# Batch 1's first DFT stage inside batch 0's pairs, V spread by matmuls, four filter parts

## The chip, the cores and the metric

The kernel runs on one core of one Trainium2 chip. The metric is the device time of one execution in microseconds (us), here the median of several runs. The profile is of one further execution.

## The reference

The input x has 8 batches of 3136 positions by 256 channels. Two blocks follow each other:

```python
X = np.fft.rfft(x, axis=1)
Y = X * (filt_r + 1j * filt_i)[None]          # 1569 frequencies x 256 channels
y = np.fft.irfft(Y, n=3136, axis=1)           # a global filter over the positions

h = y.transpose(0, 2, 1) @ U @ V              # U 3136x32, V 32x3136
u = y + h.transpose(0, 2, 1)
out = u + np.maximum(u @ w_ch1, 0) @ w_ch2    # 256 -> 1024 -> 256
```

Inputs and output are float32; the kernel computes in float16 with float32 accumulation.

## The kernel before

The 3136 positions are split as 64 q by 49 r, and the DFT is done in stages by matmuls. The first stage ("f1") is a DFT over q: matmuls of chunks of x (`xt`) with the constant `w64`. The second is a DFT over r, with twiddles, for 32 frequency groups s; it uses the table `t2` (98 rows, 128 columns for each s) and gives `px`. A pair m handles s = 2m and 2m + 1, so there are 16 pairs. VectorE (DVE) multiplies `px` by the filter tile `ft` (line 408 or lines 419 and 421, `uv`). The inverse of the second stage uses the table `g12` (`pi`); the inverse of the first one uses `s2` within `u_part`. `ft` holds the real filter rows in its first half and the imaginary rows in its second; partitions 64 to 127 get a copy of partitions 0 to 63 (`swap_filters`, line 188) and a negated copy (line 189).

Batch 0 is done at the start, on its own. `first_f1` makes the transposed first stage, `first_a` transposes it back for each pair, and `first_mid` runs the 16 pairs: the product on DVE, `back` (line 313, eight matmuls) for the pair before, `forward` two pairs ahead, `first_a` three pairs ahead. ScalarE (ACT) copies the results of `back` (line 316, `et`) and of `first_a` (line 296, `a`) out of PSUM. After the pairs comes a stage of 13 steps, called the e2 stage here: four transposes on TensorE (line 346), then a copy to `e2`, by ACT and DVE in turn (lines 350 and 352). Into each of these 13 steps one unit of batch 1's f1 is put (`next(fill)`): a matmul (line 366) and a copy by ACT or DVE (lines 372 and 370) to `asb`; after the last unit of a chunk SyncE (SP) stores the chunk in DRAM (`c1`, line 376). Two matmul steps, `h1_unit(0)` (line 467) and `make_u(0)` (lines 490 and 495), lead to the main loop.

The main loop goes over groups of four r, seven groups in an odd batch and six in an even one. Each group has eight matmul pairs `mm1` (line 527) with a ReLU (lines 532 and 534), the eight-step `mm2` of the group before (lines 549 and 553), its copy to `och` (line 558) and two stores to `out` (line 565). `make_u` of the next group stands in the middle. The other batches' DFT work is spread over this loop by slots, eight in a group of four: `put(slot, gen)` fixes which unit runs where. Batch 1's pairs start at slot 9, with `load_a(1, 0)`, the load of the stored first stage, at slot 3.

The order on every engine is the program's order (`manual_schedule`), and the DMA queues of SP and GpSimd (POOL) issue in that order too. POOL issues the loads that convert to float16: x of batch 0 (eight loads), all parts of the filters (`load_filters`, lines 162 to 179), U, x of batch 1, V, `w1`, `w2`, `s2`, x of batch 2. SP issues the tables (`load_tables`, line 157), all of them before the pairs. V is loaded four times, to partitions 0, 32, 64 and 96, in two halves, and POOL copies it to `vrs` in the order that `u_part` needs (`prep_v`, line 228).

Of the kernel before, what the change touches and what calls it, by code (L numbers as in the profile page):

```python
# [16 lines left out]
DM = 256  # L17
# [8 lines left out]
def _consts():  # L26
    n, half = SEQ, SEQ // 2
    r = np.arange(NR)
    q = np.arange(NQ)


    w = np.zeros((NQ, NS, 2))
    for s in range(NS):
        w[:, s, 0] = np.cos(2 * np.pi * s * q / NQ)
        w[:, s, 1] = -np.sin(2 * np.pi * s * q / NQ)
    w[:, 0, 1] = (-1.0) ** q
    w = w.reshape(NQ, 64)
    w64 = np.zeros((128, 128))
    w64[:64, :64] = w
    w64[64:, 64:] = w  # L40
    s2 = np.zeros((128, 128))
    s2[:64, :64] = w.T / ESC
    s2[64:, 64:] = w.T / ESC


    t2 = np.zeros((NS, 98, 128))
    g = np.zeros((NS, 128, 98))
    for s in range(NS):
        for j in range(49):
            if j < 25:  # L50
                f = s + 64 * j
                e, sg = np.exp(-2j * np.pi * f * r / n), 1.0
            elif s:
                f = 64 * (j - 24) - s
                e, sg = np.exp(-2j * np.pi * (n - f) * r / n), -1.0
            else:
                f = 32 + 64 * (j - 25)
                e, sg = np.exp(-2j * np.pi * f * r / n), 1.0
            ei = np.conj(e)
            if s:  # L60
                t2[s, :49, j], t2[s, 49:, j] = e.real, -e.imag
                t2[s, :49, 64 + j], t2[s, 49:, 64 + j] = sg * e.imag, sg * e.real
                g[s, j] = np.concatenate([ei.real, ei.imag]) * 2
                g[s, 64 + j] = np.concatenate([-ei.imag, ei.real]) * 2 * sg
            else:
                o = 0 if j < 25 else 49
                t2[s, o:o + 49, j] = e.real
                t2[s, o:o + 49, 64 + j] = e.imag
                g[s, j, o:o + 49] = ei.real * (2 if f else 1)
                g[s, 64 + j, o:o + 49] = -ei.imag * 2  # L70

    t2[0, :, 64] = 0
    t2[0, 49:, 64] = (-1.0) ** r
    g[0, 64] = 0
    g[0, 64, 49:] = (-1.0) ** r
    g *= ESC / n
    gs = np.concatenate([g[:, 64:], g[:, :64]], 1)
    f16 = np.float16
    return (w64.astype(f16), s2.astype(f16), np.eye(128).astype(f16),
            np.ascontiguousarray(t2.transpose(1, 0, 2).reshape(98, NS * 128)).astype(f16),  # L80
            np.ascontiguousarray(np.stack([g, gs], 1).transpose(2, 0, 1, 3)
                                 .reshape(128, NS * 2 * 98)).astype(f16))
# [3 lines left out]
def kernel(  # L86
# [10 lines left out]
):  # L97
    nc = tc.nc
    nb = x.shape[0]
    w64_np, s2_np, idn_np, t2_np, g_np = _consts()  # L100
    w64_d = nc.inline_tensor(w64_np, name="w64d")
    s2_d = nc.inline_tensor(s2_np, name="s2d")
    idn_d = nc.inline_tensor(idn_np, name="idnd")
    t2_d = nc.inline_tensor(t2_np, name="t2d")
    g_d = nc.inline_tensor(g_np, name="gd")
    RD = NR * DM
# [38 lines left out]
    g12 = cst.tile([128, NS * 2 * 98], F16)  # L145
    ft = cst.tile([128, 2 * NS * DM], F16)
    nyq = cst.tile([65, DM], F16)
    PARTS = ((0, 4), (4, 8), (8, 16), (16, 24), (24, 32))
    for a, b in PARTS:
        for c in (0, NS * DM):  # L150
            nc.vector.memset(ft[32:64, c + a * DM:c + b * DM], 0.0)
# [28 lines left out]
                nyq[64:65, :],  # L180
                bass.AP(tensor=filt_r.tensor, offset=(SEQ // 2) * DM, ap=[[DM, 1], [1, DM]]))

    def swap_filters(a, b):

        fb = NS * DM
        if a == 0:
            nc.vector.memset(ft[0:1, fb:fb + DM], 0.0)
        nc.vector.tensor_copy(ft[64:128, a * DM:b * DM], ft[0:64, a * DM:b * DM])
        nc.vector.tensor_scalar_mul(ft[64:128, fb + a * DM:fb + b * DM],
                                    ft[0:64, fb + a * DM:fb + b * DM], -1.0)  # L190
        if a == 0:
            nc.vector.tensor_copy(ft[64:65, 0:DM], nyq[64:65, :])

    for a, b in PARTS:
        load_filters(a, b)
    uq = sb.tile([64, NR * RANK], F16, tag="esb", bufs=2, name="uq")
    nc.gpsimd.dma_start(uq, moe_U.rearrange("(q r) p -> q (r p)", q=NQ))
    for c in range(len(CH)):
        load_x(1, c)
    vqs = []  # L200
    for k in range(2):
        v = sb.tile([128, SEQ // 2], F16, tag="och", bufs=2, name="vq")
        vqs.append(v.rearrange("p (q r) -> p r q", r=NR))
        for j in range(4):
            nc.gpsimd.dma_start(v[32 * j:32 * j + 32, :], moe_V[:, k * (SEQ // 2):(k + 1) * (SEQ // 2)])
    w1 = cst.tile([128, 2 * 1024], F16)
    nc.gpsimd.dma_start(w1, moe_w_ch1.rearrange("(h dd) c -> dd h c", h=2))
    w2 = cst.tile([128, 8 * DM], F16)
    nc.gpsimd.dma_start(w2, moe_w_ch2.rearrange("(t cc) e -> cc t e", t=8))
    s2 = cst.tile([128, 128], F16)  # L210
    nc.gpsimd.dma_start(s2, s2_d.ap())
    VR = ((0, 8), (8, NH))
    vrs = [cst.tile([128, (b - a) * 128], F16, name=f"vr{a}") for a, b in VR]

    def v_at(r):
        k = r >= VR[1][0]
        return vrs[k], (r - VR[k][0]) * 128
    usb = cst.tile([128, NH * RANK], F16)
    nc.vector.memset(usb[64:128, (NH - 1) * RANK:NH * RANK], 0.0)

    def prep_v(part):

        a, b = VR[part]
        dst = vrs[part].rearrange("p (r h q) -> p h r q", h=2, q=NQ)
        for h in range(2):
            w = min(b, NH - h) - a
            for k, v in enumerate(vqs):
                nc.gpsimd.tensor_copy(dst[:, h, 0:w, k * 32:k * 32 + 32],
                                      v[:, h * NH + a:h * NH + a + w, :])

    def new_e2(b):
        e2 = sb.tile([128, NH * DM], F16, tag="e2", bufs=2, name="e2")
# [22 lines left out]
    def first_f1():  # L255
        ne = 0
        xs = [st[0]["x"][c] for c in range(len(CH))]
        for r0 in range(0, NH - 1, 4):
            if r0 == 8:
                load_tables(*PARTS[0])  # L260
            for dh in range(2):
                pa = bank("m", "pa")
                for rr in range(4):
                    c = next(k for k in range(len(CH)) if r0 + rr < c0[k + 1])
                    o = (r0 + rr - c0[c]) * DM + dh * 128
                    nc.tensor.matmul(pa[:, rr * 128:(rr + 1) * 128], xs[c][:, o:o + 128], w64[:, :],
                                     start=True, stop=True, skip_group_check=True)
                for h in range(2):
                    dst = atv[:, dh, :, h * NH + r0:h * NH + r0 + 4]
                    src = pa.rearrange("p (r h k) -> p h k r", h=2, k=64)[:, h]  # L270
                    if ne % 2:
                        nc.vector.tensor_copy(dst, src)
                    else:
                        nc.scalar.copy(dst, src)
                    ne += 1
# [23 lines left out]
    def first_mid(fill):  # L299
# [23 lines left out]

        pxs = [ahead(0), ahead(1)]
        for m in range(NS // 2):
            for part in PARTS[1:]:
                if 2 * m == part[0]:
                    swap_filters(*part)
            uv = both_products(m, pxs.pop(0))
            if pend is not None:  # L330
                back(*pend)
# [2 lines left out]
                pxs.append(ahead(m + 2))  # L334
            if m + 3 < NS // 2:
                first_a(m + 3)
        back(*pend)
        e2 = new_e2(0)
        for n0 in range(0, NH, 2):
# [12 lines left out]
                nc.vector.tensor_copy(dst, pt[0:k, 0:w * DM])  # L352
            if n0 == 6:
                prep_u()
            next(fill)

    def f1_units(b, both):
        ne = 0
        for c in range(len(CH)):
            xt = st[b]["x"].pop(c)  # L360
            asb = sb.tile([128, 7 * DM], F16, tag="asb", bufs=4, name="asb")
            for n0 in range(0, CH[c], 2):
                w = min(2, CH[c] - n0) * DM
                k = 64 if c0[c] + n0 == NH - 1 else 128
                pf = bank("fx"[ne % 2] if b == 1 else "m", "pf")
                nc.tensor.matmul(pf[0:k, 0:w], w64[0:k, 0:k], xt[0:k, n0 * DM:n0 * DM + w],  # L366
                                 start=True, stop=True)
                dst = asb[0:k, n0 * DM:n0 * DM + w]
                if both and ne % 2:
                    nc.vector.tensor_copy(dst, pf[0:k, 0:w])  # L370
                else:
                    nc.scalar.copy(dst, pf[0:k, 0:w])  # L372
# [112 lines left out]
    def u_part(b, r0, nr, half, pm, o, dh):  # L485

        e2, h1 = st[b]["e2"], st[b]["h1"]
        k = 64 if half else 128
        v, a = v_at(r0)
        nc.tensor.matmul(pm[:, o:o + nr * k], h1[:, dh * 128:(dh + 1) * 128],  # L490
                         v[:, a:a + nr * k], start=True, stop=False,
                         skip_group_check=True)
        for rr in range(nr):
            a = (r0 + rr) * DM + dh * 128
# [41 lines left out]
    def mm2(gx, rr):  # L536
# [22 lines left out]
        if rr == nr - 1:  # L559
            for h in range(2):  # L560
                if nr == 1:
                    dst = rows(out, b - 1 + h, r0 * DM, DM)
                else:
                    dst = rows(out, b, (h * NH + r0) * DM, nr * DM)
                (nc.gpsimd if b < nb - 1 else nc.sync).dma_start(dst, och[64 * h:64 * h + 64, 0:nr * DM])  # L565

    sched = {}

# [10 lines left out]
    SB = 48  # L579

    first_f1()
    for part in PARTS[1:]:
        load_tables(*part)
    swap_filters(*PARTS[0])
    for m in range(3):
        first_a(m)
    for part in range(2):
        prep_v(part)
        for c in range(2):
            load_x(2, 2 * part + c)  # L590
    fill = f1_units(1, True)
    first_mid(fill)
    next(h1_unit(0))
    make_u(0)
# [11 lines left out]
    for b in range(1, nb):  # L606
# [4 lines left out]
        if b > 1:  # L611
            fill = f1_units(b, b == 2)
            for k in range(NF):
                put(1.2 * k if b == 2 else steps[NP * (b - 1)] - 49 + 3 * k, fill)
            for c in range(len(CH)):
                if b > 2:
                    put(steps[NP * (b - 1)] - 68 + 10 * c, one(load_x, b, c))

    slot = 0
    for gx in range(len(groups) + 1):  # L620
# [47 lines left out]
```

## Time and profile before

| | us |
|---|---|
| median of 3 runs (565.89 to 567.01) | 566.82 |
| the profiled execution | 567.93 |
| its span, first to last instruction | 566.2 |

| engine | busy us | share of the span |
|---|---|---|
| PE (matmul) | 527.5 | 93% |
| DVE | 371.4 | 66% |
| ACT | 360.1 | 64% |
| POOL | 248.7 | 44% |

The page's row of PE in 40 slices begins with 3656889 and is 9 from there to the slice before the last; a slice is 14.2 us. The granted TensorE clock is 6 tenths in the third slice and 8 in the fourth of the digits that are not 9 (9968999...), so the low digits stand near 28 to 57 us. The DMA engines are 80% busy or more through the first 70 us. A busy share counts the time in which an instruction is under way; matmuls overlap, so a busy PE is not a PE at its peak. In the views, "idle before" is the time for which the engine had nothing to do before the instruction, and behind the arrow stands what ended it.

### The profile page before, as it was taken

To read this page: it belongs to the slowest core of one execution; us is meant where nothing else is said; L and a number is where in the kernel's file an instruction comes from. 1 tells how busy PE (TensorE), PEld (TensorE's weight loads), DVE (VectorE), ACT (ScalarE), POOL (GpSimd) and SP (SyncE) were. 2 spreads that over 40 slices of the span, in tenths; PEclk is the share of its full clock that TensorE was granted. 3 is DMA by queue.
4 is the path that set the end of the run, shared out by engine and by line. 5 is a ranking of instruction groups with operands and counts; after the bars stand their busy time and mean duration, and the time that the engine had idled before them with its cause. 6 is when DMAs were issued, how large, how long until landed. Compare 5 with 4: busy or idle time off the path is not lost.

```text
span 566.2 us, 11536 instructions
## 1 busy us (share of the span) xinstructions
PE 527.5 (93%) x4403; PEld 377.0 (67%) x4403; DVE 371.4 (66%) x552; ACT 360.1 (64%) x723; POOL 248.7 (44%) x354
## 2 busy tenths in 40 slices
PE   3656889999999999999999999999999999999996
PEld 3444457767767766767677666767677767766665
DVE  7677556676787667776786567776787578424342
ACT  4546756676767686677767586677766576654441
POOL 6557422154564645554555445454444344210000
PEclk9968999999999999999999999999999999999999
DMA  8999977896797767787887667787766534541223
GB/s 151 194 152 177 246 172 155 197 239 151 167 205 168 174 174 168 183 207 173 177 216 169 138 171 181 170 206 174 170 168 135 145 100 106 133 92 50 75 75 83
DMA packets 68822, 90.41 MB, mean 160 GB/s; under 512 B 6902, under 2 KB 53978, under 8 KB 67872
## 3 DMA queue, kind: packets, MB, share of 16 engines
q0 software_dynamic: 18960, 48.60, 39.8%
q1 hardware_dynamic: 49808, 41.08, 30.3%
q8 instruction: 34, 0.56, 0.4%
q14 instruction: 20, 0.16, 0.1%
HBM read 57.99 MB, written 48.17 MB: 188 GB/s over the span
## 4 chain that ended last, share of the span: by engine, by line
PE 80%; DMA 8%; DVE 5%; ACT 2%; issue 2%; POOL 2%; SPq 0%; ACTq 0%; DVEq 0%; POOLq 0%
PE po L549 30%; PE phh L527 27%; PE pi L436 4%; PE px L400 4%; PE po L553 4%; PE pu L490 4%; PE pu L495 3%; PE pf L366 3%; DMA xt<-in_x_dram 3%; DMA ft<-in_filt_i_dram 2%; DVE uv L421 1%; DVE uv L408 1%; PE ph L467 1%; DMA e<-c 1%; ACT h L534 1%
## 5 line engine op out<-in xcount | busy, mean ns | idle before, releaser
L534 ACT ACTIVATE h<-phh 128x512 f16<-128x512 f32 (+1 forms) x350 | 186.5, 575 | 109.7 <-PE phh L527 109.6
L549 PE MATMUL po<-w,h 128*128 128x256 f16 x1568 | 203.2, 273 | 0.0
L527 PE MATMUL phh<-ut,w 128*128 128x512 f16 x768 | 197.5, 379 | 0.5 <-ACT ut L520 0.2
L424 POOL TENSOR_TENSOR y<-uv 128x512 f16<-128x512 f16 x96 | 110.5, 1151 | 149.4 <-DVE uv L421 79.2
L549 PEld LDWEIGHTS <-h 128*128 128x128 f16 x1568 | 150.0, 98 | 35.8
L421 DVE TENSOR_TENSOR uv<-px,ft 64x512 f16<-64x512 f32 x192 | 132.1, 688 | 2.6
L558 DVE COPY och<-po 128x512 f32<-128x512 f32 x96 | 66.4, 692 | 80.8 <-PE po L553 79.1
L527 PEld LDWEIGHTS <-w 128*128 128x128 f16 x832 | 74.9, 98 | 52.7 <-issue 3.0
L419 DVE TENSOR_TENSOR uv<-px,ft 128x512 f16<-128x512 f32 x96 | 66.0, 688 | 55.3 <-PE px L400 48.3
L440 ACT CAST esb<-pi 98x512 f16<-98x512 f32 x112 | 65.8, 588 | 40.3 <-PE pi L436 32.5
L565 POOL DMA_DIRECT2D out_dram<-och x84 | 45.8, 547 | 67.9 <-DVE och L558 65.2
L400 PE MATMUL px<-a,t 98*128 98x256 f16 x256 | 50.4, 280 | 6.7 <-DMA a<-c 2.4
L372 ACT CAST asb<-pf 128x512 f16<-128x512 f32 (+1 forms) x79 | 44.9, 569 | 15.9 <-PE pf L366 15.5
L520 ACT CAST ut<-pu 128x512 f16<-128x512 f32 x96 | 51.8, 598 | 2.3 <-PE pu L495 2.0
L553 PE MATMUL po<-idn,ut 128*128 128x128 f16 x384 | 52.8, 219 | 0.0
L532 DVE TENSOR_SCALAR h<-phh 128x512 f16<-128x512 f32 (+1 forms) x66 | 42.9, 649 | 14.1 <-PE phh L527 13.7
L408 DVE TENSOR_TENSOR uv<-px,ft 128x1024 f16<-128x1024 f32 x32 | 38.1, 1220 | 10.6 <-PE px L400 10.2
L495 PEld LDWEIGHTS <-e 128*128 128x128 f16 (+1 forms) x400 | 30.9, 97 | 17.7 <-issue 2.4
L490 PE MATMUL pu<-vr,h 128*128 128x512 f16 (+1 forms) x112 | 39.6, 354 | 1.3 <-ACT h L471 0.5
L553 PEld LDWEIGHTS <-ut 128*128 128x128 f16 x384 | 37.6, 98 | 4.3
L495 PE MATMUL pu<-s,e 128*128 128x128 f16 (+1 forms) x400 | 40.3, 218 | 0.0
L400 PEld LDWEIGHTS <-t 98*128 98x128 f16 x256 | 22.7, 100 | 25.0 <-issue 8.8
(69 smaller groups left out, 371.5 us busy)
## 6 DMA issues: line engine op xcount, KB each, us to landing
out_dram<-och POOLq DMA_DIRECT2D x84, 256.0 KB, 4.5
a<-c SPq DMA_DIRECT2D x28, 392.0 KB
c<-esb SPq DMA_DIRECT2D x28, 392.0 KB
xt<-in_x_dram POOLq DMA_DIRECT2D x56, 192.0 KB, 6.3
c<-asb POOLq DMA_DIRECT2D x42, 192.0 KB, 3.2
e<-c SPq DMA_DIRECT2D x28, 200.0 KB
e<-c SPq DMA_DIRECT2D x28, 192.0 KB
out_dram<-och SPq DMA_DIRECT2D x12, 256.0 KB
```

The source lines that it names most:

```text
L400: nc.tensor.matmul(px[:, sl * DM:(sl + 1) * DM], t2[:, s * 128:(s + 1) * 128], a2[:, (2 * ml + sl) * DM:(2 * ml + sl + 1) * DM], start=Tru ...
L419: nc.vector.tensor_mul(uv[:, 0:512], px[:, :], ft[:, a:a + 512])
L421: nc.vector.tensor_mul(uv[p:p + 64, 512:1024], px[q:q + 64, :], ft[q:q + 64, b:b + 512])
L424: nc.gpsimd.tensor_add(y, uv[:, 0:512], uv[:, 512:1024])
L440: nc.scalar.copy(esb[:, ml * 512:(ml + 1) * 512], pi[0:98, :])
L490: nc.tensor.matmul(pm[:, o:o + nr * k], h1[:, dh * 128:(dh + 1) * 128], v[:, a:a + nr * k], start=True, stop=False, skip_group_check=True)
L495: nc.tensor.matmul(pm[:, o + rr * k:o + (rr + 1) * k], e2[0:k, a:a + 128], s2[0:k, 0:k], start=False, stop=(rr == nr - 1), skip_group_chec ...
L527: nc.tensor.matmul(pm[:, 0:w], w1[:, dh * 1024 + t * 128:dh * 1024 + (t + 1) * 128], ut[:, dh * w:(dh + 1) * w], start=(dh == 0), stop=(dh ...
L534: nc.scalar.activation(h[:, 0:w], pm[:, 0:w], RELU)
L549: nc.tensor.matmul(po[:, o:o + DM], hs[gx, t][:, rr * 128:(rr + 1) * 128], w2[:, t * DM:(t + 1) * DM], start=(t == 0), stop=False, skip_gr ...
L553: nc.tensor.matmul(po[:, o + dh * 128:o + (dh + 1) * 128], ut[:, dh * w + rr * 128:dh * w + (rr + 1) * 128], idn[:, :], start=False, stop= ...
L558: nc.vector.tensor_copy(och[:, a:(rr + 1) * DM], po[:, 0:(rr + 1) * DM - a])
```

## The change

Four things are changed.

1. The filters come in four parts (0 to 4, 4 to 12, 12 to 20, 20 to 32) instead of five. Batch 1's first two x chunks are loaded ahead of the last part. The tables are no longer all issued before the pairs: part 1 is, part 2 after pair 0's product and part 3 after pair 4's. The real half's copy to partitions 64 to 127 of parts 1 and 2 moves from DVE to ACT, one pair ahead of its use.
2. Of batch 1's 13 f1 units ten go between batch 0's pairs 6 to 15, with ACT doing their copies, and three stay in the e2 stage. They take PSUM banks of the tag "o" instead of "f" and "x".
3. V is loaded once, in two halves of 32 partitions. Seven units (`v_units`) spread it to 128 partitions by matmuls with a selection matrix `sel` (32 by 128) that reads V with a step of 49 elements; ACT copies the result to `vr`. One unit stands in the e2 stage, six in the slots 1, 3, ..., 11 of the main loop. Batch 2's f1 units go from slots 0 to 14 to slots 4 to 17. POOL's copies (`prep_v`) are gone, and batch 2's x loads follow `s2` directly.
4. The second store of the very last group is issued by ACT instead of SP. The buffers of `asb` are three instead of four.

```diff
-    PARTS = ((0, 4), (4, 8), (8, 16), (16, 24), (24, 32))
+    PARTS = ((0, 4), (4, 12), (12, 20), (20, 32))
...
-    def swap_filters(a, b):
+    def swap_real(a, b, on):
+        (nc.scalar.copy if on else nc.vector.tensor_copy)(ft[64:128, a * DM:b * DM],
+                                                          ft[0:64, a * DM:b * DM])
+
+    def swap_imag(a, b):
         fb = NS * DM
         if a == 0:
             nc.vector.memset(ft[0:1, fb:fb + DM], 0.0)
-        nc.vector.tensor_copy(ft[64:128, a * DM:b * DM], ft[0:64, a * DM:b * DM])
         nc.vector.tensor_scalar_mul(ft[64:128, fb + a * DM:fb + b * DM],
                                     ft[0:64, fb + a * DM:fb + b * DM], -1.0)
...
-    for a, b in PARTS:
+    for a, b in PARTS[:3]:
         load_filters(a, b)
+    for c in range(2):
+        load_x(1, c)
+    load_filters(*PARTS[3])
+    for c in range(2, len(CH)):
+        load_x(1, c)
     uq = sb.tile([64, NR * RANK], F16, tag="esb", bufs=2, name="uq")
     nc.gpsimd.dma_start(uq, moe_U.rearrange("(q r) p -> q (r p)", q=NQ))
-    for c in range(len(CH)):
-        load_x(1, c)
     vqs = []
     for k in range(2):
-        v = sb.tile([128, SEQ // 2], F16, tag="och", bufs=2, name="vq")
-        vqs.append(v.rearrange("p (q r) -> p r q", r=NR))
-        for j in range(4):
-            nc.gpsimd.dma_start(v[32 * j:32 * j + 32, :], moe_V[:, k * (SEQ // 2):(k + 1) * (SEQ // 2)])
+        v = sb.tile([32, SEQ // 2], F16, tag="xt", bufs=8, name="vq")
+        vqs.append(v)
+        nc.gpsimd.dma_start(v, moe_V[:, k * (SEQ // 2):(k + 1) * (SEQ // 2)])
...
-    def prep_v(part):
...
+    def v_units():
+        for r0 in range(0, NH, 4):
+            n, nh = (4, 2) if r0 < NH - 1 else (1, 1)
+            pv = bank("m", "pv")
+            for k, v in enumerate(vqs):
+                nc.tensor.matmul(
+                    pv[:, 0:n * nh * 64].rearrange("p (r h q) -> p r h q", h=nh, q=64)
+                    [:, :, :, 32 * k:32 * k + 32],
+                    sel[:, :],
+                    bass.AP(tensor=v.tensor, offset=v.offset + r0,
+                            ap=[v.ap[0], [1, n], [NH, nh], [NR, 32]]),
+                    start=True, stop=True, skip_group_check=True)
+            nc.scalar.copy(vr[:, r0 * 128:r0 * 128 + n * nh * 64], pv[:, 0:n * nh * 64])
+            yield
...
         for m in range(NS // 2):
-            for part in PARTS[1:]:
-                if 2 * m == part[0]:
-                    swap_filters(*part)
+            for k, part in enumerate(PARTS):
+                if k and 2 * m == part[0]:
+                    if k == 3:
+                        swap_real(*part, False)
+                    swap_imag(*part)
             uv = both_products(m, pxs.pop(0))
...
             if m + 3 < NS // 2:
                 first_a(m + 3)
+            for k, part in enumerate(PARTS):
+                if k in (1, 2) and 2 * m + 2 == part[0]:
+                    swap_real(*part, True)
+                if k > 1 and 2 * m + 12 == part[0]:
+                    load_tables(*part)
+            if m >= 6:
+                next(fill)
...
-            next(fill)
+            if n0 in (10, 14, 18):
+                next(fill)
+            if n0 == 22:
+                next(vgen)
...
-            asb = sb.tile([128, 7 * DM], F16, tag="asb", bufs=4, name="asb")
+            asb = sb.tile([128, 7 * DM], F16, tag="asb", bufs=3, name="asb")
...
-                pf = bank("fx"[ne % 2] if b == 1 else "m", "pf")
+                pf = bank("o" if b == 1 else "m", "pf")
...
-                if both and ne % 2:
+                if both and ne % 2 and (b > 1 or ne >= 10):
...
-                (nc.gpsimd if b < nb - 1 else nc.sync).dma_start(dst, och[64 * h:64 * h + 64, 0:nr * DM])
+                eng = nc.gpsimd if b < nb - 1 else nc.scalar if gx + 1 == len(groups) and h else nc.sync
+                eng.dma_start(dst, och[64 * h:64 * h + 64, 0:nr * DM])
...
     first_f1()
-    for part in PARTS[1:]:
-        load_tables(*part)
-    swap_filters(*PARTS[0])
+    load_tables(*PARTS[1])
+    swap_real(*PARTS[0], False)
+    swap_imag(*PARTS[0])
+    nc.vector.tensor_copy(ft[64:65, 0:DM], nyq[64:65, :])
     for m in range(3):
         first_a(m)
-    for part in range(2):
-        prep_v(part)
-        for c in range(2):
-            load_x(2, 2 * part + c)
+    for c in range(len(CH)):
+        load_x(2, c)
     fill = f1_units(1, True)
+    vgen = v_units()
     first_mid(fill)
...
-                put(1.2 * k if b == 2 else steps[NP * (b - 1)] - 49 + 3 * k, fill)
+                put(4 + 1.1 * k if b == 2 else steps[NP * (b - 1)] - 49 + 3 * k, fill)
...
+    for k in range((NH - 1) // 4):
+        put(1 + 2 * k, vgen)
```

## The prediction

> **What bounds the kernel now.** I read the page first: PE is 93% busy over the span. The windows view then says where the other 7% is. This is PE, PEld, DVE, ACT and POOL busy in us, then the granted clock, the DMA share and GB/s:
>
> ```profile
> 25.70:29.10 3.40, 0.00 (x0) 0.00 (x0) 0.69 (x1) 0.54 (x1) 1.18 (x2) 1.00 1.02 183
> 29.10:32.50 3.40, 0.00 (x0) 0.00 (x0) 0.59 (x1) 0.00 (x0) 0.02 (x1) 0.50 1.01 145
> 32.50:35.90 3.40, 1.92 (x20) 1.85 (x21) 3.30 (x4) 0.74 (x3) 3.40 (x7) 0.50 0.82 125
> ...
> 39.40:42.80 3.40, 2.66 (x40) 2.29 (x38) 3.40 (x4) 2.86 (x9) 1.63 (x4) 1.00 1.09 210
> ...
> 63.67:71.50 7.83, 7.57 (x38) 3.35 (x38) 2.72 (x4) 7.18 (x15) 1.35 (x3) 1.00 0.93 226
> 71.50:75.00 3.50, 1.81 (x15) 1.32 (x14) 0.89 (x2) 0.82 (x2) 0.80 (x2) 1.00 1.07 236
> ```
>
> From 80 us on, PE hardly pauses. The time is lost before that: no compute engine does more than two copies from 25.7 to 31.9 while the DMA engines are full. The timeline names the waits (start, duration, operation, idle before it and what ended that):
>
> ```profile
> 31.91 0.69 DVE L189 TENSOR_SCALAR ft<-ft 64x2048 f16<-64x2048 f16 x1 [4.12 <-DMA ft<-in_filt_i_dram]
> ...
> 33.98 0.84 PE L313 MATMUL pi<-g,uv 128*128 128x98 f16 x8 [8.37 <-DVE uv L408]
> ...
> 41.02 2.35 DVE L408 TENSOR_TENSOR uv<-px,ft 128x1024 f16<-128x1024 f32 x2
> ...
> 50.24 0.55 ACT L316 CAST et<-pi 128x200 f16<-128x200 f32 x2 [0.80 <-PE pi L313]
> ...
> 60.99 0.92 PE L467 MATMUL ph<-e,usb 128*32 128x256 f16 x25 [0.45 <-ACT asb L372]
> ...
> 63.67 1.30 PE L527 MATMUL phh<-ut,w 128*128 128x512 f16 x4 [0.23 <-ACT ut L520]
> ...
> 74.38 0.38 PE L400 MATMUL px<-a,t 98*128 98x256 f16 x2 [1.69 <-DMA a<-c]
> ```
>
> So the opening is a chain: filter rows land; sixteen pairs of `first_mid`, paced by DVE (41.02 is the eleventh, pair 10); the e2 stage (50.8 to 60.99); h1 and `make_u`; main loop from 63.67. The chain view gives the wait, and the DMA view of 17.5 to 27.5 the reason (packets, MB, share of the engines):
>
> ```profile
> 18.01 13.88 DMA ft<-in_filt_i_dram
> ```
>
> ```profile
> q1 hardware_dynamic: 830, 1.77, 71.0%
> q0 software_dynamic: 840, 0.49, 36.2%
> ```
>
> Filters (q0) and tables (q1) pass packet for packet, but the tables take 1.77 MB and the filters 0.49. In the DMA view of 30 to 32.5, the tables done, q0 moves 0.33 MB in 2.5 us. The filters' last issue, at 32.48, lands 4.3 us later, at 36.75.
>
> **Part by part.** The base is the profiled execution: 567.93 us, span 566.2; the median of the timed runs is 566.82, 1.1 lower. 0.2%, about what a measurement tells from no change, is 1.1 us.
>
> *1. Filters and tables by parts.* By their shapes all tables are 2.41 MB and all filters 1.57. Today pair 4 waits until 32 for filters that pass beside 2.1 MB of tables. Afterwards parts 1 and 2 (frequencies 4 to 20) pass beside 1.2 MB. Part 1, which landed at 21.5, is 0.2 MB wider: 1.5 us more at the filters' pace alone (0.13 MB/us), 4.1 at the pace beside tables (0.049); I take 23.7, and four products with their swap end near 29. Part 2: 0.79 MB of filters at 0.13 and 1.2 of tables at 0.23 (2.27 MB moved in those 10 us) are 11.3 us from 15.5, landing near 28; ACT's copy of 1.84 puts pair 6 near 31.3, and pair 9 ends near 36. Part 3 (20 to 32) decides: before it on POOL's queue now stand four x loads of batch 1 (0.197 MB each at the 208 GB/s of 40 to 45 us: 0.95 us, 3.8 together), and on SP's queue the first c1 chunk (0.39 MB at the 338 GB/s of 62 to 64.5: 1.2). Bytes of filters and tables are the same. Some DMA slack goes (share 0.84 from 30 to 35: 0.8 us). Landing: 36.75 + 3.8 + 1.2 - 0.8 = about 41.0; I take 40.5, since the c1 chunk need not be wholly ahead. Bounds: 37 (loads overlap freely) and 46.8 (rival B). The swap of 12 rows on DVE is 1.5 x 0.69 = 1.0, so pair 10 starts at 41.5: 0.5 later than now.
>
> *2. Pairs 10 to 15.* Now 41.02 to 50.80, with a pair of swaps (1.4) between. After: six products at 1.155 start to start are 6.9, to 48.4, without swaps. ACT may be later: from the first back copy at 43.2 it has six pair copies at 0.55, two `a` copies and five f1 copies at 0.48 (7.18 us for 15 copies in the window from 63.67): 6.7, to 49.9. So -0.9. The f1 matmuls (0.22 each) ride on PE, whose share per pair is under DVE's at full clock.
>
> *3. The f1 units leave the e2 stage.* Now 10.15 us from 50.84 to 60.99, alternating e2 and asb copies. After: ACT has six e2 copies, 0.88 of usb, two f1 (0.48 and 0.37) and one vr, 5.1; DVE 4.8; with the first transposes' 0.65 and joints, 6.9. That is -3.3. Steps 1 to 3 move the loop's start to 59.5: -4.2, bounds -7 and +2.1 (rivals A and B), almost 1 us per us of part 3's landing. Next late after that landing: ACT.
>
> *Clock.* PE would idle from about 37 to 42.7. In the trace an idle from 25.7 to 34 left the clock at 0.50 until 39.4, and pairs then ran at 1.69 us start to start (35.36 to 37.05). With f1 (0.43 at that clock) PE has about 9 us from 42.7 for what follows pair 10; if the clock recovers 5.4 us after PE's restart, as there, the pairs end 0.6 to 1.3 later. The e2 stage's 8 us of matmuls at half clock (4 at full) would make it up to 1.1 longer. Of these 2.4 I count 0.4, inside the 6.9. "TensorE: Matmul & The Clock Gate", Part 1, says that one idle window of about 3.4 us halves the clock; the row fits, and by it the whole 2.4 would fall due, the sum being 2.0 worse.
>
> *4. The forward's wait.* The last c1 chunk leaves after n0 = 18, near 56.5, instead of after the stage; with up to the 7 us that it took now (62.06 to 68.9) and 5.4 for the `a` load, px has its operand by 69, and slot 9 comes near 69.5. -1.7 (0 if the x2 loads, now issued earlier, crowd it out); half of the 0.67 that px waits for DVE at 78.79: -0.3.
>
> *5. V.* Eight loads become two, and POOL's eight copies (7.9 us) go: nothing waited for them, so 0. Added: seven selection units, one in the e2 stage (in 3), six in slots 1 to 11. The first group's window shows ACT as its limit: 7.18 of 7.83, against 5.8 of matmul pace (16 x 0.216, 0.86 for `make_u`, 7 x 0.22). There ACT gets four vr copies and two f1 copies fewer: 2 x 0.48 = +1.0. Three f1 units shift into the PE-bound groups, 0.66, with two v units, 0.3. Together +2.0. No row has a moving operand that steps 98 bytes. Nearest is the contiguous one, 0.109 per 256 columns (eight in 0.87), which I take; farthest is POOL's copy of the same V at the same step, 746 ns per 256 elements (against 576 for its contiguous add, 1151 per 512). At that pace four units in the first group bring PE there from 5.2 (three f1 fewer) to 11.2, 3.0 over ACT's 8.2, and the later units cost 1.6 more: +6.6. Lower end: ACT's 0.65 idle in that window absorbs part, and two f1 units hide: +0.7. It adds work only, so no gain. "Advanced Engine Details and Errata", SBUF Cachelines, says that a read needs two hits on a 16-byte line for full pace; this one has one, which speaks against the change; taken as half pace (an estimate), the sum is 0.5 worse. No row here shows it.
>
> *6. Tail.* The last two stores issue on SP one after the other (1.60 us from 561.79). One moves to idle ACT: -0.6, between -1.0 and 0.
>
> *At nothing.* ACT's waits for the filters' real parts (1.84 us a copy by the slope from 0.38 at 256 to 0.59 at 512): behind them stand et and `a` copies, but DVE waits for the same rows; uncovered, 1.84 each. PE's f1 matmul waits for x chunks, with `back` behind it: chunks 0 and 1 land before part 3, chunks 2 and 3 near 42.4 and 44.3, in time for pairs 12 and 15; else 1 to 2. POOL waits with x2's later chunks until f1 frees buffers (pair 11, long before); behind it are c1 of batch 2, not needed until slot 25. Three asb buffers: the fourth chunk is 4 us later, a store lands in 3. Table memsets: 0.06 each.
>
> **Sum.** -4.2 - 1.7 - 0.3 + 2.0 - 0.6 = -4.8: 563.1 in a profiled execution, 562.0 on the median's scale.
>
> **Rivals.** *A, part 3 comes early.* x1 overlaps with the filters, as the share of 0.82 near 33 allows, and part 3 lands by 37.5: then the engines limit, -7: 559.2. Against: the share stood near 1.0 nearly everywhere.
> *B, slower: part 3 lands late.* Its tables (0.9 MB) are released only after pair 4, so they meet part 3 rather than passing earlier. At 0.177 MB/us (1.77 in 10 us) they take 5.1 us, and with a second c1 chunk ahead (1.2) the landing is 46.8; the loop then starts 2.1 late, the sum is +1.5: 568.3. It decides from a landing at 45.3.
> *C, the strided reads cost POOL's pace.* Then step 5 is 6.6 instead of 2.0: 566.6, no change. For: every 2-byte value is 98 bytes from the last. Against: POOL itself loses only 1.3 times by it.
>
> **Chances.** Forecast 0.58, A 0.14, B 0.14, C 0.14. Faster (below 565.7): 0.55 + 0.14 from A + 0.03 from C = 0.72. Same: 0.02 + 0.02 from B + 0.08 from C = 0.12. Slower: 0.01 + 0.12 from B + 0.03 from C = 0.16. The forecast's own range is 559.5 to 565 (landing 38 to 43.5); the whole one reaches 1.0 below A, for step 4 and 6's own bounds, and past C into B: 558.2 to 567.4.
>
> **What would show it.** Right: DVE's long wait is before pair 10 and ends at 39 to 42; L467 starts near 57, the first L527 near 59.5; px at slot 9 without a wait for `a<-c`; 17 ACT copies in the first group. Wrong: part 3 landing after 45; ph after 61; a v matmul pair over 0.9 us; a new wait of PE for an x chunk.

## The result, and the profile after

The changed kernel takes 568.4 us (median of 20 runs, 566.32 to 570.66), the kernel before 566.23 (20 runs, 564.91 to 569.04): a ratio of 1.0037, 95% interval 1.0024 to 1.0051. It is slower by 0.4%, and above the upper end of the range. The profiled execution took 568.4 us with a span of 566.6, 0.47 more than that of before.

The windows view of after, in the columns of before:

```profile
25.70:29.10 3.40, 1.38 (x11) 0.95 (x8) 1.80 (x2) 3.27 (x5) 2.36 (x4) 1.00 1.07 231
...
39.40:42.80 3.40, 3.40 (x31) 2.81 (x31) 3.37 (x4) 3.08 (x8) 0.66 (x1) 0.59 1.09 216
60.55:71.50 10.95, 10.84 (x40) 2.86 (x40) 2.08 (x3) 8.03 (x16) 0.36 (x1) 1.00 0.61 165
```

The hole from 25.7 on is filled, with ACT at 3.27 and DVE at 1.80 of 3.40. But the loop's first stretch, in which ACT was busy for 7.18 of 7.83 us before, is now PE's: 10.84 of 10.95, with ACT at 8.03. Selected rows of the timeline of after show both (DVE, ACT and PE in order of time):

```profile
22.72 0.58 PE L421 MATMUL px<-a,t 98*128 98x256 f16 x2 [3.50 <-DMA t<-t2d]
25.82 0.69 DVE L195 TENSOR_SCALAR ft<-ft 64x2048 f16<-64x2048 f16 x1 [4.62 <-DMA ft<-in_filt_i_dram]
27.99 4.64 DVE L429 TENSOR_TENSOR uv<-px,ft 128x1024 f16<-128x1024 f32 x4 [1.48 <-ACT ft L187]
33.32 0.59 PE L421 MATMUL px<-a,t 98*128 98x256 f16 x2
34.37 0.59 ACT L305 CAST a<-pt 98x512 f16<-98x512 f32 x1 [0.49 <-PE pt L303]
34.98 1.90 ACT L187 COPY ft<-ft 64x2048 f16<-64x2048 f16 x1
36.91 4.62 DVE L429 TENSOR_TENSOR uv<-px,ft 128x1024 f16<-128x1024 f32 x4 [3.56 <-ACT ft L187]
38.56 0.38 PE L421 MATMUL px<-a,t 98*128 98x256 f16 x2
43.75 2.36 DVE L429 TENSOR_TENSOR uv<-px,ft 128x1024 f16<-128x1024 f32 x2
51.85 1.07 PE L364 MATMUL pe<-idn,et 128*128 128x128 f16 x16 [0.64 <-ACT et L325]
57.85 0.94 PE L488 MATMUL ph<-e,usb 128*32 128x256 f16 x25
60.55 1.29 PE L547 MATMUL phh<-ut,w 128*128 128x512 f16 x4 [0.23 <-DMA xt<-in_x_dram]
61.77 1.27 PE L229 MATMUL pv<-vq,sel 32*128 32x256 f16 x2
73.33 0.38 PE L421 MATMUL px<-a,t 98*128 98x256 f16 x2
```

Pair 2 starts at 27.99, pair 6 at 36.91, pair 10 at 43.75 (41.02 before); the e2 stage lasts from 51.85 to 57.85, 6.0 us instead of 10.15; the loop starts at 60.55, 3.1 earlier. The px of slot 9 waits for nothing. And a pair of selection matmuls (line 229) takes 1.27 us.

The px rows also show PE's pace. A px pair takes 0.58 to 0.59 us from 22.72 to 33.32, and 0.38 at 38.56. From 29.27 to 36.0 PE has no gap, and px starts every 1.69 us (31.63, 33.32, 35.00): the pace that the prediction reads at a clock of 0.50, where DVE needs 1.16 for a product. The clock column says 1.00 for this stretch (first row of the windows view); the durations do not bear it out.

The ACT copies of `ut` are a milestone in every group, and their lead over before shows where the 3.1 us went: -3.13 in the first group, -1.10 in the second, -0.09 in the third, +0.69 in the fourth and after. So 3.8 us are lost: 2.0 before the second copy, where two selection units stand, 1.0 before the third (four units, the last a small one; before, px waited 1.69 us here), and 0.8 before the fourth. No selection unit stands in that last stretch, but three more of batch 2's f1 units (0.22 us each) do, because of their later slots: the prediction's 0.66. After that the executions differ only by two waits for loads near 320 and 382 us (-1.3 and +1.0) and by 0.1 at the end: -3.1 + 3.8 - 0.3 + 0.1 = +0.5, the 0.47 seen. The chain of waits from 55 to 75 us says by which line (first row: the lines' shares; then start, duration):

```profile
by line: PE pv L229 36.2%; PE phh L547 25.0%; PE pf L387 7.6%; PE pe L364 6.4%; ACT ut L540 5.4%; PE ph L488 4.4%; PE po L569 4.4%; PE pu L510 4.1%; PE pu L515 3.4%; ACT h L492 2.0%; PE px L421 1.1%; issue 0.9%; PE po L573 0.6%
...
61.84 1.21 PE pv L229 x2
63.05 0.97 PE phh L547 x4
```

Over a third of those 20 us is the selection matmuls, 1.21 us a pair, on the path, each longer than the four ReLU-stage matmuls next to it.

### The profile page after: what moved, and what is told of

Same layout as the page of the kernel before. It is cut to its first block, busy times and chain, and to the rows that moved or that the text cites. A ratio compares the mean times of both kernels' runs of the same rounds, so it can differ in the third digit from the quotient of the medians.

```text
span 566.6 us, 11533 instructions
## 1 busy us (share of the span) xinstructions
PE 534.7 (94%) x4417; PEld 377.8 (67%) x4417; DVE 366.6 (65%) x539; ACT 368.9 (65%) x737; POOL 235.5 (42%) x336
## 4 chain that ended last, share of the span: by engine, by line
PE 86%; DVE 4%; ACT 4%; DMA 3%; issue 2%; POOL 1%; ACTq 0%; DVEq 0%; POOLq 0%
PE po L569 30%; PE phh L547 28%; PE px L421 5%; PE pi L457 5%; PE po L573 4%; PE pu L510 4%; PE pu L515 4%; PE pf L387 3%; DVE uv L429 2%; DMA xt<-in_x_dram 1%; PE pv L229 1%; PE ph L488 1%; DVE uv L442 1%; ACT h L554 1%; DMA t<-t2d 1%
## 5 line engine op out<-in xcount | busy, mean ns | idle before, releaser
L461 ACT CAST esb<-pi 98x512 f16<-98x512 f32 x112 | 65.8, 588 | 38.5 <-PE pi L457 30.8
L586 POOL DMA_DIRECT2D out_dram<-och x84 | 45.6, 546 | 64.0 <-DVE och L578 64.0
L393 ACT CAST asb<-pf 128x512 f16<-128x512 f32 (+1 forms) x84 | 48.3, 575 | 14.8 <-PE pf L387 14.8
L552 DVE TENSOR_SCALAR h<-phh 128x512 f16<-128x512 f32 (+1 forms) x66 | 42.8, 649 | 20.7 <-PE phh L547 20.2
L136 POOL DMA_DIRECT2D xt<-in_x_dram x64 | 34.4, 545 | 15.9 <-DMA ft<-in_filt_i_dram 5.1
L397 POOL DMA_DIRECT2D c<-asb x48 | 26.1, 546 | 35.6 <-ACT asb L393 30.4
```

What stands on the lines that cost most here:

```text
L461: nc.scalar.copy(esb[:, ml * 512:(ml + 1) * 512], pi[0:98, :])
```

## The experiments

Three theories stood for the loss in the loop. **S**: the step of 49 elements at which the moving operand is read. **H**: the hand-off of each unit (a PSUM bank, a copy on ACT), whatever is read. **L**: the later slots of batch 2's first-stage units. The opening's miss (pairs end 1.0 us later than before instead of 0.9 earlier) is studied after that.

### The read by itself: e5_steps

The kernel before, with sets of 16 matmuls behind its end, alike but for the step and the rows of the moving operand.

```
for K, step in ((128, 1), (128, 2), (128, 3), (128, 4), (128, 8), (128, 16), (128, 49), (32, 1), (32, 49)):
    for i in range(16):
        matmul(pz[:, 0:256], idn[0:K, :], <ft, 256 elements at this step>)
```

> The kernel before with nine sets of sixteen matmuls behind the main loop: 256 moving columns of float16 read from the filter tile at steps of 1, 2, 3, 4, 8, 16 and 49 elements with 128 rows, and at 1 and 49 with 32 rows. Theory S: start to start 0.11 us at step 1 and about 0.5 to 0.6 at step 49, with 32 rows as with 128. Open is where it rises: if a 16-byte line must be hit twice, up to step 4 it stays at 0.11 and rises from 8 on; if it grows with the bytes spanned, 8 to 49 differ. Rival H: 0.11 at every step.

The execution takes 608.27 us with the sets behind its end; what is read are the sets. One matmul of a set from start to start, by step: 1: 0.109 us, 2: 0.115, 3: 0.172, 4: 0.228, 8: 0.452, 16: 0.460, 49: 0.548. The timeline shows four of the sets (15 or 16 matmuls of one set in a row):

```profile
559.21 1.91 PE L643 MATMUL pz128x<-ft,idn 128*128 128x256 f16 x16
562.98 2.74 PE L643 MATMUL pz128x<-ft,idn 128*128 128x256 f16 x15
569.65 6.96 PE L643 MATMUL pz128x<-ft,idn 128*128 128x256 f16 x15
584.33 8.42 PE L643 MATMUL pz128x<-ft,idn 128*128 128x256 f16 x15
```

These are steps 1, 3, 8 and 49: the contiguous read that the prediction took is a fifth of the read that the change makes. The cost rises in proportion to the step from 2 to 8 and little after that. The windows view over the sets at step 1, at step 8 (first and last part) and at step 49, and over the contiguous set of 32 rows, adds the clock (third from the end):

```profile
559.20:560.90 1.70, 1.70 (x19) 1.51 (x18) 0.42 (x1) 0.00 (x0) 0.00 (x0) 1.00 0.39 84
570.00:573.00 3.00, 3.00 (x8) 0.81 (x7) 0.00 (x0) 0.00 (x0) 0.00 (x0) 1.00 0.00 0
573.50:576.30 2.80, 2.80 (x7) 0.75 (x6) 0.00 (x0) 0.00 (x0) 0.00 (x0) 0.50 0.00 0
584.60:592.40 7.80, 7.80 (x15) 1.72 (x13) 0.00 (x0) 0.00 (x0) 0.00 (x0) 0.50 0.00 0
592.80:595.90 3.10, 3.10 (x16) 2.09 (x16) 0.00 (x0) 0.37 (x1) 0.00 (x0) 0.50 0.02 5
```

Within the set of step 8 the granted clock halves, and the matmuls go on at 0.45 us: it is the read that paces them, not the array. With 32 rows, as in the change, a matmul at step 49 takes 0.548 too. (The 32-row contiguous set, at 0.213, ran at that half clock; it does not say that 32 rows cost more.)

### The read made contiguous: e1_contig

The selection matmuls read runs of 32 neighbouring elements of V. These are not the elements that belong there, so this kernel leaves the right V out; everything else is as in the changed kernel.

```
-  ap=[v.ap[0], [1, n], [NH, nh], [NR, 32]]        # offset v.offset + r0
+  ap=[v.ap[0], [nh * 32, n], [32, nh], [1, 32]]   # offset v.offset + r0 * 32
```

> The changed kernel, with the selection matmuls reading V in one contiguous run instead of at a step of 98 bytes; the rows of V that it spreads are therefore not the right ones, everything else is the same. In the profile after, such a matmul pair holds PE for 1.2 us (61.77 to 62.98). Theory S (the step costs): the pair falls to about 0.25 us, six units in the loop give back 5 x 0.97 = 4.9 us, the ratio to before is about 0.995 (0.993 to 0.997). Rival H (the unit costs by its hand-off to ACT and its PSUM bank, whatever it reads): the pair stays over 1.0 us and the ratio stays near 1.004. Rival L (batch 2's f1 units in later slots cost the loop): as H in time, but with a short pair.

563.25 us, ratio 0.9925 (0.9899 to 0.9951): 1.1% below the changed kernel, with the same units, banks, copies and slots. The lead is 3.9 us at the first group and 4.2 from the fourth on. In the chain of 55 to 75 us the selection matmuls have all but gone and ACT is the limit again:

```profile
by line: ACT h L554 15.5%; PE phh L547 11.9%; ACT ut L540 10.3%; PE po L569 8.7%; ACT e L368 7.8%; ACT vr L236 7.2%; ACT asb L393 6.4%; DVE uv L429 6.1%; PE ph L488 4.4%; PE pf L387 4.3%; PE px L421 4.1%; issue 3.9%; PE pv L229 2.4%; PE pi 
```

S holds: H and L asked for a ratio near the changed kernel's. From the first to the fourth group the changed kernel loses 3.8 us and this one gains 0.3, so the read alone is worth 4.1 us of the loop. It shows too that the prediction's own sum for the loop was right for the read that it assumed: steps 4 and 5 together were to be 0.0, and the lead moves by 0.3.

### V's part alone, and V's part undone: e3_v_only, e2_v_pool

The kernel before with `v_units`, the single load of V and the new slots only; and the changed kernel with `prep_v` and the eight loads of V back.

> The kernel before with the V change alone: V loaded once, selection units, batch 2's f1 units in slots 4 to 17. Theory S: seven units of 1.2 us on PE, of which the forward's wait of 1.7 us hides a part: 8.4 - 1.7 = 5 to 7 us slower than before, ratio 1.009 to 1.012. Rival H: the same. If the opening's other parts and not V made the changed kernel slow, the ratio is 1.000 to 1.003.

572.73 us, 1.0091 (1.0068 to 1.0114). The loop starts 2.4 us later (one unit stands in the e2 stage, and the pairs end 0.9 later in this execution), and 6.2 by the fourth group: 3.8 us lost in the loop, as in the changed kernel. S and H both asked for this; that the opening and not V made the changed kernel slow, which asked for 1.000 to 1.003, is ruled out.

> The changed kernel with V prepared as before: eight loads and POOL's copies, no selection units; batch 2's f1 units stay in slots 4 to 17. Theory S: the loop starts near 60.6 as in the changed kernel, no unit stands in it, px does not wait; 567.9 - 3.1 - 1.7 = about 5 us under before, ratio 0.991 (0.988 to 0.994). Rival L: the loop's later slots still cost, ratio 0.996 or more. Rival H: as S.

564.34 us, 0.9949 (0.9928 to 0.9971). It wins, but less than S said. The timeline of this run has the reason:

```profile
61.53 0.58 PE L512 MATMUL pu<-s,e 128*128 128x128 f16 x4 [2.28 <-DMA s<-s2d]
...
63.64 4.55 PE L544 MATMUL phh<-ut,w 128*128 128x512 f16 x11 [0.25 <-ACT ut L537]
```

With eight loads of V ahead of it, `s2` lands at 61.5 and `make_u(0)` waits 2.28 us for it; in the changed kernel it landed at 55.0. Behind the wait the granted clock is 0.50 from 61.5 to 67, and eleven matmuls take 4.55 us where four of the same take 0.86 in the chain at 84.12: by an estimate from these rows about 2 us more, 11 x (0.41 - 0.22). In this execution the lead is 0.9 us by the fourth group; with these 4 us it would be near S's 5. So the smaller load of V, which the prediction put at 0, has a price once the e2 stage is short.

### The same elements in another order: e6_neigh, e8_v_neigh_only

Each unit needs four neighbouring r. Read them together, 64 pieces of four elements instead of 256 of one, and let the matmul scatter its columns in PSUM.

```
-  pv ... "p (r h q) -> p r h q" [:, :, :, 32 * k:32 * k + 32]
+  pv ... "p (r h q) -> p q h r" [:, 32 * k:32 * k + 32, :, :]
-  ap=[v.ap[0], [1, n], [NH, nh], [NR, 32]]
+  ap=[v.ap[0], [NR, 32], [NH, nh], [1, n]]
```

> The changed kernel with one thing altered: the selection matmuls read the same elements of V in another order, four neighbouring positions at a time (64 pieces of four for 256 columns, instead of 256 pieces of one), and scatter the columns in PSUM instead. All that is computed is unchanged. Step theory (the cost is the number of separate places that a moving operand is read from): a pair of selection matmuls falls from 1.21 us to about 0.43 us (twice the 0.213 us that 32 rows cost at step 1 in the runs by themselves), the offset to before at group 3 and later turns from +0.4..+0.7 to -3.5..-4.2, ratio to before 0.992 to 0.995, as in the run with the contiguous read (0.9925). Hand-off theory (each unit costs a PSUM bank and an ACT copy, whatever is read): as the changed kernel, 1.003 to 1.004. A third possibility: scattering the 256 columns in PSUM costs what gathering them from SBUF did; then also 1.003.

563.63 us, 0.9951 (0.9926 to 0.9976), 0.9% below the changed kernel. The pair's row in the chain:

```profile
60.74 0.53 PE pv L229 x2
```

0.53 us instead of 1.21, not the 0.43 expected, and that figure was not a good one: it is twice the 0.213 of a set at half clock. A contiguous pair in e1_contig takes 0.32 in the chain (at 69.68). The 0.2 that is left may be the pieces or the scatter in PSUM, which these runs do not separate. The lead goes from 4.2 at the first group to 3.8.

> The kernel before with part 3 of the change alone (V loaded once, units, slots), and with the read order of e6_neigh. The same part with the read of step 49 gave 1.0091. Step theory: six units of 1.2 us fall to about 0.45 us: 4.6 us off, so 572.7 - 4.6 = 568, ratio 1.000 to 1.003 (six units of 0.45 us added to PE in the loop, some gain from V's smaller load). Hand-off theory: 1.009 again.

568.91 us, 1.0038 (1.0019 to 1.0057), a little above the 1.000 to 1.003 expected. Against e3_v_only the read order alone is worth 0.5%. But V's part does not pay even so on its own. Why is not shown: its profiled execution, 566.86, is the fastest of its ten, and there the loop starts 0.1 earlier than before and is 0.35 late by the fourth group. A likely reading is that its gain, `s2` early, needs a short e2 stage. Against e6_neigh the other parts of the change are worth 0.87%, 4.9 us.

### The units back in the e2 stage: e9_neigh_f1_late

e6_neigh with `next(fill)` out of the pairs and into all 13 steps, with the banks and the DVE copies of before.

> As e6_neigh, but batch 1's first-stage units all go back to the e2 stage, one in each step, with DVE and ACT in turn and the banks of before: part 2 of the change undone, the rest kept. If the forecast of step 3 was right (the shorter e2 stage carries the gain), the e2 stage lasts 9.5 to 10.2 us instead of 6.0 and the pairs end 0 to 0.5 us earlier: loop start 3.3 to 4 us later, ratio 0.006 to 0.007 above e6_neigh (0.999 to 1.001). If the e2 stage's length was set by something else (DVE or ACT alone, or w1 and s2 landing), the ratio stays within 0.002 of e6_neigh.

569.77 us, 1.0065 (1.0044 to 1.0085): 1.1% above e6_neigh. The PE rows of its timeline bound the e2 stage, and DVE's names a wait in it:

```profile
50.53 0.61 PE L362 MATMUL pe<-idn,et 128*128 128x128 f16 x4 [0.64 <-ACT et L325]
...
59.63 0.69 DVE L388 CAST asb<-pf 128x512 f16<-128x512 f32 x1 [0.68 <-DMA c<-asb]
...
62.22 0.93 PE L485 MATMUL ph<-e,usb 128*32 128x256 f16 x25 [0.48 <-ACT asb L390]
```

11.7 us, against 5.5 in e6_neigh (51.25 to 56.75): part 2 of the change is what pays here. The stage is longer than before's 10.15: it holds a selection unit as well, and three `asb` buffers instead of four make it wait for a store of `c1`. So 1.1% is somewhat more than part 2 alone is worth. Some of it is the clock: 0.53 from 50 to 53 us here, 1.00 through the stage in e6_neigh.

### The opening: e7_neigh_dve, e11_five_atonce, e10_five_released, e13_five_late

e7_neigh_dve gives the real half's copies of parts 1 and 2 back to DVE, in e6_neigh.

> As e6_neigh, and the real half's copies of parts 1 and 2 are given back to DVE, at the same place of the program. If pair 6 waited for ACT's place in the order (36.91 us, with part 2 landed at 30.26 and ACT's copy begun only at 34.98), it starts at 33.5 to 35 now, but pair 10 still waits for part 3, which landed at 41.86 and needs 2.2 us of swaps: pair 10 at 43.4 to 43.8, loop start no earlier by more than 0.3 us, ratio to before the same as e6_neigh within 0.0010. If instead pair 10's time was set by the chain of DVE's own work from pair 6 on, all of the gain passes on: loop start 1.5 us earlier than e6_neigh, ratio 0.0026 lower.

564.92 us, 0.997 (0.9954 to 0.9986). DVE's timeline:

```profile
33.63 4.62 DVE L429 TENSOR_TENSOR uv<-px,ft 128x1024 f16<-128x1024 f32 x4
42.70 0.95 DVE L187 COPY ft<-ft 64x3072 f16<-64x3072 f16 x1 [4.45 <-DMA ft<-in_filt_r_dram]
44.19 0.95 DVE L195 TENSOR_SCALAR ft<-ft 64x3072 f16<-64x3072 f16 x1 [0.54 <-DMA ft<-in_filt_i_dram]
```

Pair 6 starts 3.3 us earlier than in the changed kernel and 2.9 earlier than in e6_neigh, so ACT's place in the order was what it waited for; and then DVE waits 4.45 us for part 3, the wait that the prediction put there. With it comes the prediction's clock term: PE stands for 5.16 us before 46.53, the granted clock is 0.50 from 45.6 to 52, and px pairs start every 1.94 us (47.16, 49.09, 51.03). In this execution, the slowest of its twelve, the loop starts 3.9 us later than in e6_neigh. By the medians nothing is gained: two limits lay one behind the other.

The next three take e6_neigh with the filters in before's five parts, all ahead of batch 1's x, and their copies on DVE; eight of batch 1's units go beside pairs 8 to 15 and five in the e2 stage. e11_five_atonce issues all tables before the pairs, as before; e10_five_released issues the last three parts after pairs 0, 2 and 6.

> As e10_five_released, but with all the tables issued before the pairs, as before: part 1 of the change undone, the rest kept. Pairs as in e8_v_neigh_only: the last one's copy done at 50 to 50.5 us, the e2 stage 6.6 to 7.2 us, so the loop starts within 0.5 us of e6_neigh's, ratio to before 0.994 to 0.997. A difference between this run and e10_five_released is the worth of releasing the tables by parts: by the landing theory 1 to 2 us.

564.5 us, 0.9968 (0.9946 to 0.9989).

> As e6_neigh, with the opening rebuilt: the filters in the five parts of before and all ahead of batch 1's x, the real half's copies on DVE right before their pair, the tables of the three later parts still released one by one (after pairs 0, 2 and 6), batch 1's units beside pairs 8 to 15 (eight) and in five steps of the e2 stage. If the pairs are paced by the landing of the filters (part 8 to 16 landed at 31.9 us before, behind all the tables; the changed kernel's own part 2 at 30.3, then x and part 3 at 41.9), that part lands at 28 to 30 us, pair 4 starts at 29.5 to 31.5 instead of 32.7, the last part is no longer waited for, and the pairs end at 48 to 49.6; the e2 stage takes 6.6 to 7.2 us with five units; loop start 1.2 to 2.5 us earlier than in e6_neigh, ratio to before 0.990 to 0.993. If the pairs are paced by DVE's work or the tables' late release is what is waited for, the ratio is 0.994 to 0.997, no better than e6_neigh.

562.74 us, 0.9919 (0.9894 to 0.9944), the lowest ratio of the study: faster than the kernel before and than the changed one. Against e11_five_atonce, releasing the tables is worth 0.3% by the medians and 0.5% by the ratios, whose intervals only just part. The DMA view of 17.5 to 27.5 us of e10_five_released, beside the one in the prediction, shows why (packets, MB):

```profile
q0 software_dynamic: 1349, 0.82, 66.7%
q1 hardware_dynamic: 483, 0.99, 38.5%
```

On POOL's queue, the filters', 0.82 MB pass instead of 0.49, beside 0.99 of tables instead of 1.77. Pair 4 starts at 25.8 us, 6.9 earlier than before. Its timeline shows what takes 3.5 of them back:

```profile
38.61 0.59 PE L381 MATMUL pf<-xt,w 128*128 128x512 f16 x1 [3.95 <-DMA xt<-in_x_dram]
...
40.31 1.23 DVE L423 TENSOR_TENSOR uv<-px,ft 128x1024 f16<-128x1024 f32 x1 [3.54 <-PE px L415]
```

The first unit stands in PE's order before x has landed, and the products wait behind it. PE then goes on at a granted clock of 0.50 (38.5 to 42 us). e13_five_late begins the units at pair 12, with nine in the e2 stage.

> As e10_five_released, with batch 1's units begun four pairs later: four beside pairs 12 to 15, nine in the e2 stage. In e10_five_released PE stood for 3.95 us at 38.61 us before the first of these units, whose x chunk had only just landed, and the products on DVE stood for 3.54 us behind it. If that wait can be bought off, the pairs end 2.5 to 3.9 us earlier and the e2 stage with nine units instead of five takes 1.2 to 2 us more: loop start 1 to 2.5 us earlier than in e10_five_released, ratio to before 0.987 to 0.991. If w1 and s2 (landed at 53.9 and 54.1) or ACT's copies are next late, nothing comes of it: 0.991 to 0.994.

562.55 us, 0.9941 (0.9915 to 0.9967): not told apart from e10_five_released, so no better. The pairs end 4.4 us earlier, and the e2 stage gives it back:

```profile
45.47 0.40 PE L358 MATMUL pe<-idn,et 128*128 128x128 f16 x4 [0.64 <-ACT et L322]
...
52.33 0.69 DVE L385 CAST asb<-pf 128x512 f16<-128x512 f32 x1 [1.84 <-DMA c<-asb]
...
56.18 1.68 PE L482 MATMUL ph<-e,usb 128*32 128x256 f16 x25
```

It starts at 45.47 and lasts 10.7 us, with nine units and a wait of 1.84 for an `asb` buffer. Behind that wait the granted clock is 0.50 from 56 to 59, and the 25 matmuls of the last row take 1.68 us instead of 0.94. A fourth buffer was not tried.

### The small parts: e12_neigh_slots

e6_neigh with batch 2's units back in slots 0 to 14 and the very last store back on SP.

> As e6_neigh, with batch 2's first-stage units back in slots 0 to 14 and the last store back on SP: two small parts of the change undone. Step theory: neither matters, ratio within 0.002 of e6_neigh's 0.9951. Slot theory (the later slots cost or spare something): the offset to before, read at the copies of ut, differs from e6_neigh's -3.8 by over 0.8 us at groups 1 to 3. The ACT store: end minus last copy 5.3 to 5.4 us with either engine.

565.13 us, 0.997 (0.9955 to 0.9986): not told apart from e6_neigh's 0.9951. The lead in the loop is 3.4 and later 3.2 instead of 3.8, so in these two executions the later slots spare about half a microsecond rather than cost any, and L falls here too. (The stretch from the third to the fourth copy of `ut` is 12.03 us with the early slots and 12.80 with the later ones; the stretches ahead of it make up for that.) From the start of the last DVE copy to the end it is 5.3 us, as in the kernel before, and 5.4 with the store on ACT.

## Why the prediction was wrong, by its own steps

**Step 5, the term that failed.** "Nearest is the contiguous one, 0.109 per 256 columns (eight in 0.87), which I take": so the term became +2.0. e5_steps gives 0.548 for that read alone, the changed kernel 0.6 (1.21 a pair). In the loop the term is 3.8 for steps 4 and 5 together where 0.0 was said; since step 4 came (below), step 5 is about 5.8. By e1_contig the read's share is 4.1 of it, and the 1.7 that is left is near the 2.0 said. This is rival C's mechanism, near its price (0.746 per 256, +6.6), and the prediction's marker "a v matmul pair over 0.9 us" is the row that shows it. What misled was the choice between two ends: the contiguous row was nearest in engine and shape, but not in the thing that differs, the step; and POOL's small loss by the same step spoke only for an engine that takes over four times as long for its contiguous elements and could hide the read. The Trainium skill, "Advanced Engine Details and Errata", SBUF Cachelines, spoke against the change rightly; the prediction's reading of it as half pace was too mild. Its rule of two hits on a line differs from these runs too: step 4 still has two elements in 16 bytes and costs 0.228, 2.1 times the contiguous read.

**Steps 1 and 2, too early by 1.1 us at the loop's start with step 3.** Part 1's landing was put at 23.7 and came at 25.7, its tables held px until 22.72, and pair 2 started only at 27.99. Pair 2, too, waited for ACT: 1.48 us for a real copy that began at 26.06, behind an `a` copy. Part 2 landed at 30.3 (28 was said, though its own terms, 15.5 + 11.3, give 26.8), but its real copy stands on ACT behind the `a` copy of pair 8. That one waits for PE's transposes (34.37, 0.49), and PE ran these pairs at half pace, so the real copy began at 34.98 and pair 6 at 36.91 instead of 31.3. The prediction counted 1.84 for that copy and not its place in the order; e7_neigh_dve shows the place. In e6_neigh, whose opening is the same and where a px pair takes 0.38 from 33.39 on, pair 6 starts at 36.57, 0.3 earlier; what the half pace costs in all was not measured. Part 3's landing was right (40.5 said, 41.9 came), yet decided nothing here, since DVE was busy until 41.53: rivals A and B, which hang on it, did not come up. The forecast of DVE's long wait was wrong by place: it lies before pairs 2 and 6. From pair 10 to the last `et` copy it is 8.05 us where 8.4 was said.

**Step 3, right.** 6.9 said, 6.0 measured, and e9_neigh_f1_late undoes it for 1.1%. A part of it is not in the sum: before, the clock was 0.50 from 50 to 53 us, at the start of the stage, and here it is 1.00 throughout.

**Clock, due at another place.** The prediction put PE's idle time, and the half clock behind it, before pair 10. There it did not come: PE idles for 2.19 us before 38.19, behind that the clock is 0.59 of full speed from 39.4 to 42.8, while DVE paced the pairs, and it is 1.00 through the e2 stage and the loop's start, so the 2.4 us did not fall due. But PE starts at half pace in both kernels (px pairs of 0.58 to 0.59 us). Before, it is at 0.42 by 22.21; in the changed kernel it stands for 3.50 us before 22.72 and 2.17 before 29.27, and pairs 2 to 5 run at half pace. The rule of the Trainium skill, "TensorE: Matmul & The Clock Gate", Part 1, that an idle window of about 3.4 us halves the clock, agrees with e7_neigh_dve (5.16 us of idle PE, then 0.50); but in the changed kernel 0.50 follows the 2.19 us, and in e2_v_pool 2.28.

**Step 4, right**: px at slot 9 waits for nothing; before, the chain from 55 to 75 us had 27.1% of `a<-c`. **Step 6, wrong**: -0.6 said; the start of the last copy to the end is 5.4 us against 5.3 before, so the issue of the last store was not what the end waits for. What it does wait for was not followed. **At nothing**: V's smaller load was put at 0; e2_v_pool shows 2.28 us of wait for `s2`, and a half clock behind it, when the eight loads come back.

Together: -3.1 for the loop's start where -4.2 was said, +3.8 where 0.0 was said, +0.1 where -0.6 was said, and -0.3 of load waits that differ between executions.

## What to carry to other kernels

Before a gather is moved from an idle engine to the one that bounds the kernel, price its read pattern on that engine: a few rows of matmuls behind the end of the kernel gave the number that no row of the profile had, and reading the same elements in runs of four instead of one took 0.9% off. A load released in parts is worth it only if what follows its landing stands early enough in its engine's order, here ACT's copy and PE's first x matmul. Ask of every wait of PE what pace it leaves behind: after 5.16, 3.95 and 2.28 us of it the clock was 0.50 for some us in three of these kernels. And when a stretch is shortened, ask again what was free beside it: `s2`'s landing cost nothing until the e2 stage had become 4 us shorter.

## What the hardware showed that was not expected

- A float16 moving operand of 128 rows and 256 columns costs 0.109 us at step 1, 0.115 at step 2, 0.172 at step 3, 0.228 at step 4, 0.452 at step 8, 0.460 at step 16, and only 0.548 at step 49.
- At step 8 this cost does not depend on the granted clock: it was 0.45 us at clock 1.00 and at 0.50.
- The clock was granted at half while PE was busy without a gap by the profile, 4 us after matmuls at step 8 began (569.2 to 573.2 us). By the rule on idle windows in the Trainium skill, "TensorE: Matmul & The Clock Gate", Part 1, it would have been held. That a PE waiting for its reads counts as idle would explain it, but this was seen in one execution only, and a cause is not shown.
